# Layer-norm sums of tile 2 on ScalarE, the fourth input tile ahead of wv, and the last k norm in halves: one change to a fused attention and MLP kernel

## The chip, the core and the metric

The kernel runs on one core of one Trainium2 chip. The time is the device time of one launch in microseconds (us); the figure used is the median over several runs. An engine is called as in the profile: PE is TensorE (PEld its weight loads), DVE is VectorE, ACT is ScalarE, POOL is GpSimd, SP is SyncE, which here only issues DMAs.

## What is computed

The input x has 2048 tokens of 448 features in bf16. It is normalised, and two branches run on the normalised x:

```
xn  = layernorm(x)                                  # eps 1e-5, no scale or bias
# branch A, 16 heads of 28
q, k, v = split(xn @ wqkv)
phi(t)  = concat(softmax(t @ w_phi), softmax(-t @ w_phi))
kv = sum over tokens of phi(k)^T v ;  z = sum over tokens of phi(k)
A  = (phi(q) kv / (phi(q) z + 1e-6)) @ wo
# branch B
h  = gelu(layernorm(xn) @ w1)
hs = (h with its four column quarters shifted by -1, +1, -2, +2 tokens) @ w2
x1 = xn + hs
B  = x1 + gelu(layernorm(x1) @ w3) @ w4
out = x + A + B
```

Since xn is already normalised, the kernel uses it for both branches' first products.

## The kernel before

**Tiles.** The tokens are 16 tiles of 128. `xtok` holds x, `xn` the normalised x with tokens on the partitions, `xnT` its transpose with features on the partitions. The 448 features of a contraction lie in four overlapping chunks of 128, so that a matmul uses 64 rows of PE and two matmuls on the upper and the lower 64 rows run side by side; a "pair" below is such a couple. Where the upper rows write a bank after the lower rows did, PE waits for its own earlier matmul.

**Order.** Nothing is scheduled automatically. A `Recorder` notes every operation in the order of the program, gives each engine its own instruction queue in that order, and sets semaphores where a tile is written and read. So the order in which lines are written is the order on each engine's queue. Helpers record the operations, so most rows of the profile carry a helper's line: L200 is a matmul, L204 a PE transpose, L208 an ACT instruction with one output, L212 an element-wise instruction, L215 a transposing DMA, L218 a DMA, L807 a sum on ACT.

**Loads (L354 to 364).** x tiles 0, 2 and 3 are issued by SP, tile 1 by ACT; then the two halves of `wv` (the v columns of wqkv, contraction chunks 0, 1 and 2, 3), the first by ACT and the second by SP; then the further x tiles, two or four at a time, `w1`, `w_phi` and transposing loads of wqkv, all on SP.

**Head (L794 to 830).** A tile is normalised in steps: mean and variance by `ln_stats` (bn_stats and bn_aggr on DVE); the variance plus eps; to the power -1/2 on POOL (`ln1_pow`); and one DVE instruction that subtracts the mean and multiplies (`ln1_apply`). Tile 1 is treated otherwise: ACT forms the mean (Copy with a running sum) and the mean square (Square with a running sum) by `ln1_sum`, DVE computes mean squared minus eps, POOL subtracts it from the mean square, then the power. PE meanwhile runs `spin`: matmuls of 256 columns on constant data whose result is not used, 18 ahead of the transposes of tile 0 and 5 behind them. `xn_T(i, b)` transposes tile i by eight small matmuls into bank pair b, and ACT (for some tiles DVE) copies the result to `xnT`.

**First part of v (L534 to 555, L869).** `v_pair(i, b)` computes v for tiles i and i+1. It returns three steps: early (index 0), late (1) and mid (2). `V(i, 0)` is one pair of matmuls of chunk 0, `V(i, 2)` the other three, `V(i, 1)` the six matmuls that cross over to the other bank; for i above 3 the early step holds the mid step too. The order on PE is: tile 2's transposes, V(0,0), tile 3's transposes, V(0,2), V(0,1), V(2,0), V(2,2), then the first products with w1.

**Norm of k (L634 to 646) and kv (L648, L662, L667).** For a couple of tiles, `k_norm` sums the exponentials of each head on DVE, takes the reciprocal, and POOL multiplies all of both tiles in one instruction over 128 x 1792 (L643). The last call, for tiles 14 and 15, first has DVE apply the second layer norm to tiles 4 and 5 (`g_apply`, and after the norm `g_T`, a transposing DMA). `kv_tile(i)` is 16 matmuls of 62 columns on PE that add tile i to kv in banks 6 and 7. `kv_copy` (DVE) folds the two banks, `kv_blocks` (PE, then DVE and ACT) lays kv out for the products with phi(q).

**Later part (L930 to 985).** A list written by hand interleaves steps on PE: `a(p)` and `b(p)` are the early (8 matmuls of 512 columns) and late (6) half of a product with w3, followed by a gelu on ACT; `K(...)` calls kv_tile; `w2_last` finishes the last product with w2; `N(i)` multiplies phi(q) of tile i with kv; `f(n, k)` are the steps of the final product; `S` stores; `A` and `G` call g_apply and g_T. The part of interest reads:

```
a(0), (wl[11][0],), b(0), a(1), K(10, 11), b(1), K(12), a(2), K(13), b(2), a(3), K(14, 15), b(3), (kv_copy,),
a(4), (w2_last, 11), b(4), a(5), (kv_blocks,), b(5),
a(6), N(0), ...
```

Of the kernel before, what the change touches and what calls it, by code (L numbers as in the profile page):

```python
# [5 lines left out]
ACT = mybir.ActivationFunctionType  # L6
ALU = mybir.AluOpType
# [4 lines left out]
LN_EPS = 1e-5  # L12
# [208 lines left out]
def bass_parallel_sum__linear_kernel_hedgehog__mixer_s_mlp__prompt_kernel(  # L221
    nc, A_x, A_wqkv, A_w_phi, A_wo, B_x, B_w1, B_w2, B_w3, B_w4, out,
):
    _, S, D = A_x.shape
    H, DH = A_w_phi.shape[0], A_w_phi.shape[1]
# [10 lines left out]
    with es:  # L236
        R = Recorder(nc, es)
# [9 lines left out]
        def view(h, cols, dt=BF16, at=0):  # L247
            a = h[:, at // 2:at // 2 + cols * DTB[dt] // 2]
            return a if dt == BF16 else a.bitcast(dt)

        def new(name, cols, dt=BF16):
            return view(region(name, cols * DTB[dt]), cols, dt)
# [9 lines left out]
        xtok = new("xtok", NT * D).rearrange("p (t d) -> p t d", t=NT)  # L262
# [14 lines left out]
        wv = new("wv", KC * D).rearrange("p (c d) -> p c d", c=KC)  # L277
# [11 lines left out]
        g_tok = view(g_r, 4 * 512).rearrange("p (b d) -> p b d", b=4)  # L289
# [8 lines left out]
        st = new("st", NT * 8, F32).rearrange("p (t c) -> p t c", t=NT)  # L298
        mv = new("mv", NT * 8, F32).rearrange("p (t c) -> p t c", t=NT)
        rs = new("rs", NT * 8, F32).rearrange("p (t c) -> p t c", t=NT)  # L300
        st2 = new("st2", NT * 8, F32).rearrange("p (t c) -> p t c", t=NT)
# [38 lines left out]
        dve, pool = "DVE", "POOL"  # L340


        def load_x(i, n, eng="SP"):
            R.dma(xtok[:, i:i + n, :], x2d[128 * i:128 * (i + n), :].rearrange("(j p) d -> p j d", p=128), eng)
# [5 lines left out]
        def load_lap(dst, src, engs=("SP", "SP")):  # L350
            for h in range(2):
                R.dma(dst[:, 2 * h:2 * h + 2, :], src[192 * h:192 * h + 256, :].rearrange("(c p) d -> p c d", p=128), engs[h])
# [1 line left out]
        load_x(0, 1)  # L354
        load_x(1, 1, "ACT")
        load_x(2, 1)
        load_x(3, 1)
        load_lap(wv, A_wqkv[:, 896:1344], ("ACT", "SP"))
        load_x(4, 2)
        load_x(6, 2)  # L360
        load_lap(w1, B_w1)
# [66 lines left out]
        def lap(a):  # L428
            return bass.AP(a.tensor, a.offset, [list(a.ap[0]), [192, 2], [1, 256]])

        def halves(a):
            return a.rearrange("p (b e) -> p b e", b=2)

        def ln_stats(stt, mvt, src, i):
            R.ew(dve, "bn_stats", stt[:, i, 0:6], src[:, i, 0:D])
            R.ew(dve, "bn_aggr", mvt[:, i, 0:2], stt[:, i, 0:6])
# [8 lines left out]
        def ln_apply(eng, dst, src, mvt, rst, i):  # L445
            m, op = (mvt[:, i, 0:1], ALU.subtract) if eng == dve else (rst[:, i, 1:2], ALU.add)
            R.ew(eng, "tensor_scalar", dst, src, m, rst[:, i, 0:1], op0=op, op1=ALU.mult)
# [6 lines left out]
        def ln1_apply(eng, i):  # L454
            ln_apply(eng, halves(xn[:, i, :]), lap(xtok[:, i, :]), mv, rs, i)
# [3 lines left out]
        def spin(n, cols):  # L459
            for _ in range(n):  # L460
                R.mm(banks[7][:, 0:cols], busy[:, 0:128], busy[:, 0:cols], True, True)
# [49 lines left out]
        LO, HI = (0, 64), (64, 128)  # L511

        def row_pairs(first, second, start=False, cols=1):
            for s, (p, q) in enumerate(zip(first, second)):
                for out, lhs, rhs in (p, q) if cols == 1 else (*p, *q):
                    R.mm(out, lhs, rhs, start and s == 0, False)
# [17 lines left out]
        def v_pair(i, b):  # L534
            def side(k, rows, kcs):
                lo, hi = rows
                return [(banks[2 * b + k][:, 0:D], xnT[lo:hi, kc, 128 * (i + k):128 * (i + k) + 128], wv[lo:hi, kc, :])
                        for kc in kcs]

            def early():  # L540
                row_pairs(side(0, LO, (0,)), side(1, HI, (0,)), True)
                if i > 3:
                    mid()

            def mid():
                row_pairs(side(0, LO, (1, 2, 3)), side(1, HI, (1, 2, 3)))
            return early, lambda: row_pairs(side(1, LO, (0, 1, 3)), side(0, HI, (0, 2, 3))), mid

        def v_out(i, b, eng="ACT"):
# [56 lines left out]
        def w2_pair(i, b):  # L606
            def side(k, j, rows):
                lo, hi = rows
                t, r = i + 4 * j, []
                for c in range(3):  # L610
                    c0 = HB + 128 * t - SHIFTS[lo > 0][c]
                    r.append((banks[2 * b + j][:, 0:D], hT[lo:hi, c, c0:c0 + 128], w2[lo:hi, c, :]))
                if k:
                    c0 = 128 * (t % 4) + 2
                    r.append((banks[2 * b + j][:, 0:D], hD[lo:hi, t // 8, c0:c0 + 128], w2[lo:hi, 3, :]))
                return r
            return (lambda: row_pairs(side(1, 0, LO), side(1, 1, HI), True),
                    lambda: row_pairs(side(0, 1, LO), side(0, 0, HI)))
# [15 lines left out]
        def k_norm(i, between=()):  # L634
            ph = phik[:, i:i + 2, :, 0:DH].rearrange("p t g e -> p (t g) e")
            r = 2 * (i // 2 % 2)
            k, rk = (t[:, r:r + 2, :].rearrange("p b c -> p (b c)") for t in (ksum, rks))
            R.ew(dve, "tensor_reduce", k, ph, axis=AX.X, op=ALU.add)
            R.ew(dve, "reciprocal", rk, k)
            for j in between:  # L640
                g_apply(j, dve)
            rb = rk.unsqueeze(2).to_broadcast([128, 4 * H, DH])
            R.op(pool, lambda e: e.tensor_tensor(ph, ph, rb, op=ALU.mult), [ph],  # L643
                 [ph, rk, *(g_tok[:, j % 4, :] for j in between)])
            for j in between:
                g_T(j)

# [34 lines left out]
        def g_apply(i, eng="POOL"):  # L682
            ln_apply(eng, halves(g_tok[:, i % 4, :]), lap(xn[:, i, :]), mv2, rs2, i)

        def g_T(i):
            j = 128 * (i % 4)
            R.dma_t(gT[:, (i // 4) % 2, :, j:j + 128], g_tok[:, i % 4, :])
# [106 lines left out]
        def play(fs):  # L794
            for f in fs:
                f[0](*f[1:])

        def ln1_pow(j, at):
            R.ew(pool, "tensor_tensor", rs[:, j, 0:1], mv[:, j, at:at + 1], mhalf[:, 0:1], op=ALU.pow)

        def ln1_eps(j):
            R.ew(dve, "tensor_scalar", mv[:, j, 2:3], mv[:, j, 1:2], LN_EPS, 1.0, op0=ALU.add, op1=ALU.mult)
            ln1_pow(j, 2)

        def ln1_sum(j, func, scale, acc, junk):
            out, in_ = xn[:, junk, 0:D], xtok[:, j, :]
            R.op("ACT", lambda e: e.activation(out, in_, func, scale=scale, accum_out=acc), [out, acc], [in_])  # L807

        sq = st2[:, 1, 0:1]
        ln1_sum(1, ACT.Copy, 1.0 / D, mv[:, 1, 0:1], 14)  # L810
        ln1_sum(1, ACT.Square, D ** -0.5, sq, 15)
        ln_stats(st, mv, xtok, 0)
        ln1_eps(0)
        R.ew(dve, "tensor_scalar", mv[:, 1, 2:3], mv[:, 1, 0:1], mv[:, 1, 0:1], -LN_EPS, op0=ALU.mult, op1=ALU.add)
        R.ew(pool, "tensor_tensor", mv[:, 1, 4:5], sq, mv[:, 1, 2:3], op=ALU.subtract)
        ln1_pow(1, 4)
        ln_stats(st, mv, xtok, 2)
        ln1_apply(dve, 0)
        ln1_eps(2)
        ln_stats(st, mv, xtok, 3)  # L820
        ln1_apply(dve, 1)
        ln1_eps(3)
        ln1_apply(dve, 2)
        ln1_apply(dve, 3)
        spin(18, 256)
        play([(xn_T, 0, 0), (spin, 5, 256), (xn_T, 1, 1)])
        for i in range(4, 10):
            ln1_stats(i, 1, 0)
            if i > 4:
# [63 lines left out]
        side = [12, 0, 1, 2, 3, 8, 9, 10]  # L893
# [34 lines left out]
        wl = {i: w2_pair(i, 2) for i in (11,)}  # L928

        def a(p):  # L930
            return (w3p[p][0],)

        def b(p):
            return (w3p[p][1],)

        def f(n, k):
            return (fp[k][n - 1],)

        def N(i):
            return (lambda: (num_tile(i), o_T(i)),)  # L940

        def K(*t):
            return (lambda: [kv_tile(i) for i in t],)
# [5 lines left out]
        def G(*t):  # L949
            return (lambda: [g_T(i) for i in t],)  # L950
# [4 lines left out]
        def A(*t):  # L955
            return (lambda: [g_apply(i) for i in t],)

        play([
            (ln_scale, mv2, rs2, 6, 2, 0), (g_apply, 6, dve), (g_apply, 7, dve), G(6, 7),
            a(0), (wl[11][0],), b(0), a(1), K(10, 11), b(1), K(12), a(2), K(13), b(2), a(3), K(14, 15), b(3), (kv_copy,),  # L960
            a(4), (w2_last, 11), b(4), a(5), (kv_blocks,), b(5),
            a(6), N(0), (w2_norm, 8), b(6), a(7), f(1, 0), b(7), N(1), (w2_norm, 10), A(8, 9, 10, 11),
            a(8), f(2, 0), b(8), G(8, 9), a(9), N(2), (w2_norm, 12), b(9),
            a(10), f(3, 0), b(10), f(4, 0), G(10, 11),
# [51 lines left out]
```

The softmax here doesn't subtract the row's maximum and nothing guards it: scores larger than these inputs give would overflow.

## Time and profile before

| what | us |
|---|---|
| median of 5 runs | 174.1 (174.07 to 174.38) |
| the profiled execution's own time | 174.07 |
| its span (first to last instruction) | 172.3 |
| around the span | 1.8 |
| busy PE / DVE / POOL / ACT | 168.0 / 111.9 / 91.2 / 83.3 |
| first real transposes on PE (tile 0) | 5.55 |
| transposes of tiles 1, 2, 3 | 6.67, 7.05, 7.90 |
| V(0,0), V(0,2), V(0,1) start | 7.18, 8.03, 8.83 |
| POOL's norm of k tiles 14 and 15 | 71.32 to 74.53 |
| K(14, 15) on PE | 74.59 |

Times in the profile count from the start of the span. A row gives the start, the length, the engine, the line of the kernel, the operation, the tile written and the tiles read, the shapes, how many instructions of the kind follow one another, and, in brackets, how long the engine stood idle before and what ended that. The matmuls of PE are pipelined and their ends are modelled, so neighbouring rows overlap; starts are the safer figure. [...]

### The profile page before, as it was taken

What the parts mean: (1) busy time and instruction counts of PE and PEld (TensorE: products, weight loads), DVE (VectorE), ACT (ScalarE), POOL (GpSimd) and SP (SyncE); (2) the same over time, 40 slices, a digit from 0 to 9 for tenths busy, and PEclk for the clock granted to TensorE, in tenths of its full rate; (3) what the DMA queues carried; (4) which work ended last, traced back from release to release, by engine and by line L of the source; (5) the groups of instructions that cost most, each with busy time, mean ns of one, the idle gap of its engine ahead of it and who ended that gap; (6) DMA issues with size and microseconds to landing.
All of it is one profiled execution on the core that took longest, in us unless ns stands there. A gap on an engine that the chain in (4) does not pass through costs nothing.

```text
span 172.3 us, 5209 instructions
## 1 busy us (share of the span) xinstructions
PE 168.0 (98%) x2267; PEld 89.7 (52%) x2267; DVE 111.9 (65%) x260; ACT 83.3 (48%) x98; POOL 91.2 (53%) x128
## 2 busy tenths in 40 slices
PE   7899999999999999999999999999999999999994
PEld 5455576544555554544545555545545555545553
DVE  4899975278999999846677963446417425474621
ACT  4568874988778877847225322224204222224000
POOL 3576570025799999750649389540721614523740
PEclk9999999999999999999999999999999999999999
DMA  5994642229942011122103732034411220313331
GB/s 158 346 226 79 130 105 50 46 42 382 376 139 55 13 30 30 34 46 49 30 4 66 90 63 60 27 88 99 87 30 55 61 57 4 84 30 34 84 88 53
DMA packets 32679, 15.21 MB, mean 88 GB/s; under 512 B 23952, under 2 KB 32016, under 8 KB 32656
## 3 DMA queue, kind: packets, MB, share of 16 engines
q1 hardware_dynamic: 32096, 14.51, 34.3%
q8 instruction: 18, 0.29, 0.7%
q10 hardware_dynamic: 560, 0.37, 0.7%
q14 instruction: 5, 0.04, 0.1%
HBM read 7.14 MB, written 1.84 MB: 52 GB/s over the span
## 4 chain that ended last, share of the span: by engine, by line
PE 94%; DVE 3%; issue 1%; ACT 0%
PE bank L200 93%; PE bank L204 1%; DVE st L212 1%; DVE vaug L212 1%; DVE mv L212 1%; ACT xnT L208 0%; DVE xn L212 0%; DVE gT L212 0%
## 5 line engine op out<-in xcount | busy, mean ns | idle before, releaser
L208 ACT ACTIVATE phik<-bank 128x1024 bf16<-128x1024 f32 (+1 forms) x44 | 42.3, 984 | 60.4 <-PE bank L200 60.3
L200 PE MATMUL bank<-gT,w 64*128 64x512 bf16 x392 | 50.0, 377 | 0.0
L212 DVE TENSOR_TENSOR vaug<-bank,vaug 128x464 f32<-128x464 f32 (+3 forms) x65 | 32.7, 512 | 22.5 <-PE bank L200 20.9
L200 PE MATMUL bank<-w,phik 64*128 64x448 bf16 (+3 forms) x434 | 45.2, 343 | 0.0
L212 POOL TENSOR_TENSOR xnT<-vaug 128x196 bf16<-128x196 f32 (+1 forms) x32 | 18.1, 586 | 45.8 <-DVE vaug L212 45.8
L200 PEld LDWEIGHTS bank<-w,phik 64*128 64x128 bf16 (+1 forms) x434 | 22.5, 94 | 20.8 <-issue 0.4
L643 POOL TENSOR_TENSOR phik<-phik,rks 128x1792 bf16<-128x1792 bf16 x8 | 25.6, 3215 | 11.1 <-DVE rks L212 10.3
L200 PEld LDWEIGHTS bank<-gT,w 64*128 64x128 bf16 x392 | 17.6, 94 | 17.5 <-ACT phik L208 0.4
L212 POOL TENSOR_TENSOR vaug<-xn,xtok 128x448 f32<-128x448 bf16 x16 | 16.2, 1032 | 0.2 <-DVE vaug L212 0.2
L212 DVE TENSOR_REDUCE ksum<-phik 128x64 f32<-128x1792 bf16 x8 | 16.1, 2012 | 0.0
L212 DVE RECIPROCAL vaug<-bank 128x16 f32<-128x16 f32 x16 | 4.1, 257 | 17.9 <-PE bank L200 17.9
L212 POOL TENSOR_TENSOR rs<-mv,mhalf 128x1 f32<-128x1 f32 (+2 forms) x20 | 13.2, 661 | 3.5 <-DVE mv L212 2.1
L200 PE MATMUL bank<-xnT,wpq 64*128 64x512 bf16 x112 | 14.7, 376 | 0.0
L200 PE MATMUL bank<-wv,xnT 64*128 64x448 bf16 x112 | 13.6, 350 | 0.2
L200 PE MATMUL bank<-wo,xnT 64*128 64x448 bf16 (+3 forms) x110 | 13.6, 343 | 0.0
L200 PE MATMUL bank<-w,hT 64*128 64x448 bf16 x112 | 13.2, 349 | 0.0
L200 PE MATMUL bank<-wpk,xnT 64*128 64x448 bf16 x112 | 13.2, 349 | 0.0
L200 PE MATMUL bank<-xnT,w 64*128 64x512 bf16 (+2 forms) x168 | 13.0, 306 | 0.0
L212 DVE TENSOR_TENSOR xn<-bank,xn 128x512 bf16<-128x512 f32 (+1 forms) x16 | 9.2, 620 | 2.9 <-PE bank L200 2.9
L212 DVE BATCH_NORM_STATS2 st<-xn 128x6 f32<-128x448 bf16 x16 | 9.3, 581 | 0.0
L212 POOL TENSOR_SCALAR g_tok<-xn,rs 128x512 bf16<-128x512 bf16 x12 | 9.1, 769 | 0.3
L212 DVE BATCH_NORM_STATS2 st<-xtok 128x6 f32<-128x448 bf16 x15 | 9.2, 615 | 0.0
(68 smaller groups left out, 162.9 us busy)
## 6 DMA issues: line engine op xcount, KB each, us to landing
w<-in_B_w_dram SPq DMA_DIRECT2D x2, 896.0 KB, 5.8
out_dram<-vaug SPq DMA_DIRECT2D x15, 112.0 KB, 1.9
w<-in_B_w_dram SPq DMA_DIRECT2D x1, 1568.0 KB, 11.2
xtok<-in_A_x_dram SPq DMA_DIRECT2D x2, 448.0 KB, 5.8
xtok<-in_A_x_dram SPq DMA_DIRECT2D x2, 224.0 KB, 4.2
w<-in_B_w_dram SPq DMA_DIRECT2D x2, 224.0 KB, 4.5
wo<-in_A_wo_dram SPq DMA_DIRECT2D x2, 224.0 KB, 6.9
xtok<-in_A_x_dram SPq DMA_DIRECT2D x3, 112.0 KB, 2.8
```

The costliest lines, as they stand in the source:

```text
L200: self.op("PE", lambda e: e.matmul(out, lhsT, rhs, start=start, stop=stop, skip_group_check=True), [out], [lhsT, rhs], tile=self._tile(lhsT))
L204: self.op("PE", lambda e: e.transpose(out, in_, ident), [out], [in_, ident], tile=self._tile(in_))
L208: self.op("ACT", lambda e: e.activation(out, in_, func, **kw), [out], [in_] + aps)
L212: self.op(eng, lambda e: getattr(e, name)(out, *args, **kw), [out], aps)
L643: R.op(pool, lambda e: e.tensor_tensor(ph, ph, rb, op=ALU.mult), [ph], [ph, rk, *(g_tok[:, j % 4, :] for j in between)])
```

## The change

Five edits:

- x tile 3 is issued by ACT as its second load; both halves of wv are issued by SP.
- The sums of tile 2 are formed on ACT, right behind those of tile 1; `ln_stats` of tile 2 goes. `ln1_var` collects the three steps that follow such sums. On DVE, tile 3's stats stand where tile 2's stood, and tile 2's step of `ln1_var` stands behind the apply of tile 1. The unused outputs of the four sums go to rows 12 to 15 of `xn`.
- 20 spins ahead of tile 0's transposes and 2 behind them, for 18 and 5.
- For V(0, .) and V(2, .), the early step holds chunks 0 and 1 (four matmuls), the mid step chunks 2 and 3. For the other couples the sequence of matmuls is unchanged.
- In the last `k_norm`, POOL's multiply is two instructions of 128 x 896, tile 14 and then tile 15. K(14) stays behind a(3); K(15) moves behind a(4), and kv_copy behind it.

```diff
-        load_x(3, 1)
-        load_lap(wv, A_wqkv[:, 896:1344], ("ACT", "SP"))
+        load_x(3, 1, "ACT")
+        load_lap(wv, A_wqkv[:, 896:1344])
...
             def early():
-                row_pairs(side(0, LO, (0,)), side(1, HI, (0,)), True)
+                row_pairs(side(0, LO, (0, 1)), side(1, HI, (0, 1)), True)
...
             def mid():
-                row_pairs(side(0, LO, (1, 2, 3)), side(1, HI, (1, 2, 3)))
+                row_pairs(side(0, LO, (2, 3)), side(1, HI, (2, 3)))
...
-            R.op(pool, lambda e: e.tensor_tensor(ph, ph, rb, op=ALU.mult), [ph],
-                 [ph, rk, *(g_tok[:, j % 4, :] for j in between)])
+            for h in ((slice(0, 2 * H), slice(2 * H, 4 * H)) if between else (slice(0, 4 * H),)):
+                R.op(pool, lambda e, h=h: e.tensor_tensor(ph[:, h, :], ph[:, h, :], rb[:, h, :], op=ALU.mult),
+                     [ph[:, h, :]], [ph[:, h, :], rk, *(g_tok[:, j % 4, :] for j in between)])
...
-        sq = st2[:, 1, 0:1]
-        ln1_sum(1, ACT.Copy, 1.0 / D, mv[:, 1, 0:1], 14)
-        ln1_sum(1, ACT.Square, D ** -0.5, sq, 15)
+        def ln1_sums(j):
+            ln1_sum(j, ACT.Copy, 1.0 / D, mv[:, j, 0:1], 13 + j)
+            ln1_sum(j, ACT.Square, D ** -0.5, st2[:, j, 0:1], 11 + j)
+
+        def ln1_var(j):
+            R.ew(dve, "tensor_scalar", mv[:, j, 2:3], mv[:, j, 0:1], mv[:, j, 0:1], -LN_EPS, op0=ALU.mult, op1=ALU.add)
+            R.ew(pool, "tensor_tensor", mv[:, j, 4:5], st2[:, j, 0:1], mv[:, j, 2:3], op=ALU.subtract)
+            ln1_pow(j, 4)
+
+        ln1_sums(1)
+        ln1_sums(2)
         ln_stats(st, mv, xtok, 0)
         ln1_eps(0)
-        R.ew(dve, "tensor_scalar", mv[:, 1, 2:3], mv[:, 1, 0:1], mv[:, 1, 0:1], -LN_EPS, op0=ALU.mult, op1=ALU.add)
-        R.ew(pool, "tensor_tensor", mv[:, 1, 4:5], sq, mv[:, 1, 2:3], op=ALU.subtract)
-        ln1_pow(1, 4)
-        ln_stats(st, mv, xtok, 2)
+        ln1_var(1)
+        ln_stats(st, mv, xtok, 3)
         ln1_apply(dve, 0)
-        ln1_eps(2)
-        ln_stats(st, mv, xtok, 3)
         ln1_apply(dve, 1)
+        ln1_var(2)
         ln1_eps(3)
         ln1_apply(dve, 2)
         ln1_apply(dve, 3)
-        spin(18, 256)
-        play([(xn_T, 0, 0), (spin, 5, 256), (xn_T, 1, 1)])
+        spin(20, 256)
+        play([(xn_T, 0, 0), (spin, 2, 256), (xn_T, 1, 1)])
...
-            a(0), (wl[11][0],), b(0), a(1), K(10, 11), b(1), K(12), a(2), K(13), b(2), a(3), K(14, 15), b(3), (kv_copy,),
-            a(4), (w2_last, 11), b(4), a(5), (kv_blocks,), b(5),
+            a(0), (wl[11][0],), b(0), a(1), K(10, 11), b(1), K(12), a(2), K(13), b(2), a(3), K(14), b(3),
+            a(4), K(15), (kv_copy,), (w2_last, 11), b(4), a(5), (kv_blocks,), b(5),
```

## The prediction

> **What bounds the kernel now.** I read the page first: busy shares, then the chain that ended last, then the waits of TensorE and of its weight loads, then each engine's instructions in order of time in the two stretches that the diff touches.
>
> ```profile
> PE 168.0 (98%) x2267; PEld 89.7 (52%) x2267; DVE 111.9 (65%) x260; ACT 83.3 (48%) x98; POOL 91.2 (53%) x128
> PE 94%; DVE 3%; issue 1%; ACT 0%
> 8.83 2.36 PE bank L200 x22
> 26.11 143.93 PE bank L200 x1900
> ```
>
> TensorE (PE) is 98% busy, the chain is 94% PE, and after 8.83 us it is PE without a break. From there every microsecond that PE loses or saves moves the end. Before 8.83 PE waits for the first four token tiles to be normalised; the chain there runs through VectorE (DVE), GpSimd (POOL) and the copies of ScalarE (ACT). The change touches that head and one short place at 74 us. The head, engine by engine:
>
> ```profile
> 4.42 0.56 POOL L212 TENSOR_TENSOR rs<-mv,mhalf 128x1 f32<-128x1 f32 x1 [1.76 <-DVE mv L212]
> 4.95 0.19 POOL L212 TENSOR_TENSOR mv<-st,mv 128x1 f32<-128x1 f32 x1
> 5.21 0.70 POOL L212 TENSOR_TENSOR rs<-mv,mhalf 128x1 f32<-128x1 f32 x1
> 6.75 0.65 POOL L212 TENSOR_TENSOR rs<-mv,mhalf 128x1 f32<-128x1 f32 x1 [0.33 <-DVE mv L212]
> ...
> 5.48 0.62 DVE L212 BATCH_NORM_STATS2 st<-xtok 128x6 f32<-128x448 bf16 x1
> 6.23 0.38 DVE L212 TENSOR_SCALAR xn<-xtok,mv,rs 128x512 bf16<-128x512 bf16 x1
> 6.53 0.15 DVE L212 TENSOR_SCALAR mv<-mv 128x1 f32<-128x1 f32 x1
> 6.59 0.41 DVE L212 TENSOR_SCALAR xn<-xtok,mv,rs 128x512 bf16<-128x512 bf16 x1
> 7.44 0.41 DVE L212 TENSOR_SCALAR xn<-xtok,mv,rs 128x512 bf16<-128x512 bf16 x1 [0.44 <-POOL rs L212]
> ...
> 7.90 0.17 PEld L204 LDWEIGHTS bank<-ident,xn 64*128 64x128 bf16 x8 [0.16 <-DVE xn L212]
> 8.82 1.06 PEld L200 LDWEIGHTS bank<-wv,xnT 64*128 64x128 bf16 x14 [0.50 <-PE bank L200]
> ```
>
> (Start, length, engine, line, tiles; in brackets idle time before and who ended it.) Each tile needs a power on POOL (0.54 to 0.70) and an apply on DVE (0.38 to 0.41). Tile 3's apply (7.44 to 7.85) releases its transposes at 7.90, these release the six V matmuls of V(0,2) at 8.03, and V(0,1) must wait for those to drain: the last pair starts at 8.41, V(0,1) at 8.83, so a bank hand-over of 0.41. At 8.83 dense work starts, with 14 matmuls of tiles 0 to 3 still to do.
>
> **The head after the change.** DVE loses tile 2's bn_stats and bn_aggr, about 0.75 on its queue; ACT gains two sums. ACT is idle from 4.70 to 5.89; at the rows of tile 1 (0.56 each, with 0.19 to read a sum) the new pair ends at 5.80, just before its first copy at 5.89, so it costs nothing; without that gap it would push the copies by up to 1.1. Tile 3's stats move from 5.48 to 4.37, if x3 has landed: as third load of SP it took 3.4 from its issue at 1.72; as second of ACT at 1.26, beside x2 (2.8), I put it at 4.1 to 4.7. Behind bn_stats 3 stand only two short steps until 5.9, so 0.3 late costs nothing. wv's first half, now third on SP, lands 0.1 to 0.7 after its 4.46, and its first reader runs past 7. SP still issues four loads before x4, so nothing behind them on the two queues moves.
>
> The chain, with the gaps of the rows above: POOL's power of tile 1 stays at 5.21 to 5.91, since the subtraction before it and its cause do not change. Apply 1 follows 0.04 later: 5.95 to 6.33, where it was 6.23. That is a gain of 0.28 for tile 1. But tile 2's variance now stands behind apply 1 on DVE: its small multiply runs 6.25 to 6.40 (a start 0.09 before the end of the instruction ahead, as in the row at 6.53), POOL's subtraction 0.08 later, 6.48 to 6.67, its power 6.75 to 7.29 (0.54, no apply beside it). Queued behind that on POOL is tile 3's power, 7.26 to 7.92 (0.65, apply 2 beside it). On DVE, apply 2 runs 7.33 to 7.74, where it was 6.59 to 7.00, and apply 3 7.96 to 8.37 against 7.44 to 7.85. So the earlier stats of tile 3 buy nothing: POOL now does five steps in a row behind a DVE instruction that was not on the path before, and the last two tiles are late by 0.74 and 0.52.
>
> PE: transposes of tile 2 at 7.79, V(0,0) with four matmuls instead of two at 7.92, transposes of tile 3 at 8.42, V(0,2) with four at 8.55. Its second pair starts 0.19 later, 8.74, and the hand-over of 0.41 puts V(0,1) at 9.15. Behind it stand 6, 4 and 4 matmuls, 14 as before. The loss is 9.15 - 8.83 = **0.32**. The two matmuls moved ahead of tile 3 save 0.19 of the 0.52. With every power at 0.54 it is 0.22; with 0.70 for both late powers and some slower step, 0.50. I take 0.32: the rows with the same neighbours.
>
> DVE's later queue starts 0.51 late (bn_stats 4 at 7.76) while PE is 0.32 late. From 9.9 to 18.6 DVE has no pause, so the lag stays, but the smallest margin of a tile, apply 11 (ends 18.59) before its transposes at 19.14, is 0.55, above the 0.19 of difference. That costs nothing; with margin gone it would be 0.19.
>
> The spins: two more ahead, three fewer behind tile 0. The first 18 end at 5.28 and the first transposes start at 5.56. The spacing of the first is (4.02 - 0.42) / 17 = 0.21, so two more end at 5.70 at the worst and push tile 0 by 0.15, which tile 1's wait until 6.38 hides.
>
> **The kv part.**
>
> ```profile
> 71.32 3.21 POOL L643 TENSOR_TENSOR phik<-phik,rks 128x1792 bf16<-128x1792 bf16 x1 [0.85 <-DVE g_tok L212]
> 74.24 0.38 PE L200 MATMUL bank<-gT,w 64*128 64x512 bf16 x2
> 74.59 0.20 PE L200 MATMUL bank<-vaug,phik 64*128 64x62 bf16 x2
> 74.59 0.51 PEld L200 LDWEIGHTS bank<-vaug,phik 64*128 64x128 bf16 x32 [0.47 <-POOL phik L643]
> ```
>
> A pair of 512 columns takes 0.216 (74.02 to 74.24), so tiles 14 and 15 could start at 74.45 and start at 74.59: a stall of 0.14, ended by POOL's norm. In halves, tile 14's is done at about 71.32 + 1.61 = 72.93 and tile 15's at 74.5 to 74.7. K(14) then starts at 74.45; K(15), behind six and eight more matmuls, near 76.2. Both find their data. The second POOL instruction costs 0 to 0.1, and the scale behind it on POOL, the two g applies on DVE and their gT loads are as late; their readers come past 82. kv_copy, before at 76.28 behind those applies, now waits for K(15), whose last pair starts at 76.40: copy from about 76.63, its second half ends at 78.08, and the blocks are wanted at 78.3: 0.2 to spare. The two w2_out adds follow to 79.14, the CASTs that N(0) needs end at 79.9, N(0) loads at 80.03. The saving is **0.14**; if one of those two covers fails, 0 down to a loss of 0.1.
>
> **The sum.** 0.32 - 0.14 = 0.18 on a profiled run of 174.07 (span 172.3 and 1.8 around it), which is at the low end of the five times; on the median of 174.1 I get 174.3. With all ends: 0.22 - 0.15 = +0.07 to 0.50 + 0.1 = +0.6.
>
> **Rivals.**
>
> (1) PE's clock falls back. The spins of the first stretch are 0.21 apart, those at 5.78 (0.72 - 0.27) / 4 = 0.11: PE began at half pace and was fast from about 5.2. From 5.2 to 8.6 before, its array worked about 2.0 of 3.4: five spins 0.55, V 0.94, transposes 0.5. After the change I count 1.3: spins 0.37, V 0.43, transposes 0.5, with a hole from 6.5 to 7.79. If that is too little, PE runs at half pace again in the dense part. The first slow stretch lasted 3.95 from the first spin; half of it is lost, 2.0, of which about 0.3 lies beside waits (the hand-over at 8.8): 1.7. Time 176.0. For it: the thinner stretch, at the only place with such a hole. Against: no trace here shows how thin is too thin, and the granted clock stands at 1.00 throughout. It decides if the array's share between 5.2 and 8.6 is below the limit.
>
> [...]
>
> (2) The loss is absorbed. After 8.83 weight loads still wait for others, at 12.95 (0.15), 15.20 (0.44), 20.89 (0.17), 24.53 (0.29) and 26.64 (0.17). If those partners keep their times, a PE that comes 0.3 late waits 0.3 less there, and the kv gain stays alone: 174.1 - 0.14 = 173.95; with powers that run faster than their rows, or a stall at 74 that was larger than its 0.14, 173.7. Against: most partners are fed by PE itself and slide with it.
>
> (3) The head loses nothing at all because POOL takes tile 3's power ahead of tile 2's. The instruction order of the changed kernel rules it out: subtraction, power 2, power 3.
>
> **How the numbers follow.** A measurement of this kernel tells about 0.2%, 0.35 us, from no change. My forecast, a net of +0.05 to +0.6, gets 0.44: 0.24 of it below +0.35 and 0.20 above, since the ends of the head's terms lie on the slow side. The clock 0.34. The absorbed loss 0.22, half of it faster by 0.35 and half within. Faster 0.11, same 0.24 + 0.11 = 0.35, slower 0.20 + 0.34 = 0.54. The likeliest single case is 174.3, its own range 174.1 to 174.7; the whole range 173.8 to 176.1 takes in the clock.
>
> **What would show it.** Right: apply 2 near 7.3 and apply 3 near 7.95 with POOL before both, V(0,1) at 9.15, no wait at 74.5, kv_copy after K(15). Clock: pairs of 448 columns 0.37 apart instead of 0.19 somewhere past 8. Wrong: V(0,1) at or before 8.83 would fell the head's sum; a CAST that ends after 80.0, or a wait of N(0), would fell the kv gain.

## The result, and the profile after

| | before | after |
|---|---|---|
| median, us | 174.19 (173.94 to 176.14, 46 executions) | 175.61 (174.11 to 176.25, 26 executions) |
| ratio after / before, 95% interval | | 1.0052 (1.0035 to 1.0069) |
| profiled execution: own time / span / granted clock | 174.07 / 172.3 / 1.00 | 176.2 / 174.3 / 0.99 |

The change makes the kernel slower, by 0.35 to 0.69%. The median says little about how, because the 26 executions fall into two groups with nothing between. 11 took 174.11 to 174.42 (median 174.31) with PE's mean granted clock at 1.00. 15 took 175.57 to 176.25 (median 175.84) with the clock at 0.99. The ratio lies near that of the averages (175.19 against 174.28), as do the ratios below, which leave out the few executions over 1.5% above the fastest of their kernel; the median lies in the larger group. Of the 46 executions before, one is as long, and of the 91 of before that ran beside the experiments four show a clock of 0.99 or less: before does it too, but rarely. The profiled execution of after is one of the 15. The same parts of its page as were shown of before, and the row of the clock:

```profile
span 174.3 us, 5212 instructions
PE 169.0 (97%) x2266; PEld 90.1 (52%) x2266; DVE 111.5 (64%) x258; ACT 84.5 (48%) x102; POOL 91.5 (52%) x130
...
PEclk9969999999999999999999999999999999999999
...
PE 94%; DVE 2%; issue 1%; POOL 1%
```

PE still bounds the kernel, and its busy time has grown by 1.0 for the same work. The third slice of the clock, 8.7 to 13.1, reads 6: for part of it, up to 11.45, PE was granted half its pace (0.50 in the clock record). Now the head, engine by engine (columns as in the prediction):

```profile
5.27 0.70 POOL L212 TENSOR_TENSOR rs<-mv,mhalf 128x1 f32<-128x1 f32 x1
...
6.62 0.19 POOL L212 TENSOR_TENSOR mv<-st,mv 128x1 f32<-128x1 f32 x1 [0.65 <-DVE mv L212]
6.89 1.06 POOL L212 TENSOR_TENSOR rs<-mv,mhalf 128x1 f32<-128x1 f32 x2
...
5.68 0.19 ACT L808 ACTIVATION_READ_ACCUMULATOR xn<-xtok 128x1 f32 x1
5.95 0.60 ACT L208 ACTIVATE xnT<-bank 128x512 bf16<-128x512 bf16 x1
...
6.01 0.41 DVE L212 TENSOR_SCALAR xn<-xtok,mv,rs 128x512 bf16<-128x512 bf16 x1 [0.45 <-POOL rs L212]
6.34 0.27 DVE L212 TENSOR_SCALAR mv<-mv 128x1 f32<-128x1 f32 x2
7.47 0.93 DVE L212 TENSOR_SCALAR xn<-xtok,mv,rs 128x512 bf16<-128x512 bf16 x2 [0.87 <-POOL rs L212]
...
7.94 0.35 PE L204 MATMUL bank<-ident,xn 64*128 64x64 bf16 x8 [1.18 <-DVE xn L212]
10.06 0.13 PEld L200 LDWEIGHTS bank<-wv,xnT 64*128 64x128 bf16 x4 [0.86 <-PE bank L200]
```

POOL stands idle for 0.65 until DVE, behind apply 1 (6.01), has multiplied tile 2's mean (6.34). Then it forms both late powers in one row (6.89, two in 1.06), and the applies of tiles 2 and 3 follow as one row from 7.47 to 8.40. PE has nothing for 1.18 before tile 2's transposes at 7.94. V(0,1) starts only at 10.06, after a hand-over that took 0.86 instead of 0.50.

The windows view gives, for a stretch of time: its length; busy time of PE, PEld, DVE, ACT and POOL with the number of instructions; granted clock; DMA share; GB/s. Of after:

```profile
4.60:8.00 3.40, 1.60 (x28) 0.81 (x27) 1.94 (x8) 2.46 (x8) 2.55 (x6) 1.00 1.05 335
8.00:11.40 3.40, 3.34 (x32) 1.33 (x34) 3.07 (x9) 1.19 (x2) 1.53 (x5) 0.51 1.22 338
11.40:14.80 3.40, 3.40 (x52) 1.75 (x48) 3.30 (x10) 2.47 (x4) 2.67 (x7) 0.99 0.59 106
```

and of before:

```profile
4.60:8.00 3.40, 2.73 (x41) 1.29 (x40) 2.89 (x11) 1.70 (x5) 2.40 (x5) 1.00 1.06 349
8.00:11.40 3.40, 3.33 (x49) 1.60 (x48) 3.07 (x9) 1.65 (x4) 2.00 (x6) 1.00 1.22 285
```

After a stretch in which PE was busy for 1.60 of 3.40 (2.73 before), it ran at clock 0.51 for the next 3.4: 32 matmuls, where before did 49 in that stretch and after did 52 in the 3.4 behind it. In the trace's clock record the half pace lasts from 8.04 to 11.45. (The rows that start at 4.60 flatter before: its clock rose at 5.21, that of after at 4.62, and up to there spins started 0.21 apart, behind it 0.11. The section on the prediction counts the work itself.) The kv part of after:

```profile
73.21 3.35 POOL L644 TENSOR_TENSOR phik<-phik,rks 128x896 bf16<-128x896 bf16 x2 [0.85 <-DVE g_tok L212]
...
76.14 0.48 PEld L200 LDWEIGHTS bank<-vaug,phik 64*128 64x128 bf16 x16
76.58 1.19 PEld L200 LDWEIGHTS bank<-gT,w 64*128 64x128 bf16 x14
77.89 0.48 PEld L200 LDWEIGHTS bank<-vaug,phik 64*128 64x128 bf16 x16
...
78.53 0.68 DVE L212 COPY w<-bank 128x496 f32<-128x496 f32 x1
80.97 0.79 DVE L212 CAST kvq<-bank 32x232 bf16<-32x232 f32 x2
```

The halves take 3.35 together, against 3.21 in one, and neither K(14) nor K(15) has idle time ahead of it.

**The sum of the profiled execution.** Tile 0's bn_stats, which need x0, did not start at the same time in the two executions (3.30 before, 3.35 after), so the head is counted from there.

| step, from the starts of the rows | change, us |
|---|---|
| later start of tile 0's bn_stats | +0.05 |
| to the first product with w1 (6.86 before, 8.71 after) | +1.85 |
| from there to the first product with w3 | 0.00 |
| from the first product with w3 to K(14) (7.29, 7.16) | -0.13 |
| wait for a transposed o tile late in the run, 160.78 below | +0.33 |
| sum, against 172.16 - 170.06, the starts of the last instruction on DVE | +2.10, against +2.10 |

The first products with w1, of before and of after, and the wait late in after:

```profile
10.16 1.03 PE L200 MATMUL bank<-xnT,w 64*128 64x512 bf16 x8
12.06 1.02 PE L200 MATMUL bank<-xnT,w 64*128 64x512 bf16 x8
...
160.78 0.49 PEld L200 LDWEIGHTS bank<-wo,xnT 64*128 64x128 bf16 x7 [0.42 <-DMA xnT<-xnT]
```

This last wait differs between executions: the transposing DMA of that tile took 4.4 to land here, 4.2 in experiment 3 (a wait of 0.2), 3.7 in before and 3.2 in experiment 1, whose products did not wait. Of the 1.85, the next section shows 0.31 to be the lateness of tiles 2 and 3 and 1.54 the half pace.

### The profile page after: what moved, and what is told of

Read it like the earlier page. It is cut to its first block, busy times and chain, and to the rows that moved or that the text cites. A ratio compares the mean times of both kernels' runs of the same rounds, so it can differ in the third digit from the quotient of the medians.

```text
span 174.3 us, 5212 instructions
## 1 busy us (share of the span) xinstructions
PE 169.0 (97%) x2266; PEld 90.1 (52%) x2266; DVE 111.5 (64%) x258; ACT 84.5 (48%) x102; POOL 91.5 (52%) x130
## 4 chain that ended last, share of the span: by engine, by line
PE 94%; DVE 2%; issue 1%; POOL 1%
PE bank L200 93%; PE bank L204 1%; POOL rs L212 1%; DVE vaug L212 1%; DVE xn L212 0%; DVE mv L212 0%; DVE st L212 0%; POOL mv L212 0%; DVE gT L212 0%
## 5 line engine op out<-in xcount | busy, mean ns | idle before, releaser
L644 POOL TENSOR_TENSOR phik<-phik,rks 128x1792 bf16<-128x1792 bf16 (+1 forms) x9 | 25.8, 2876 | 11.1 <-DVE rks L212 10.3
L212 POOL TENSOR_TENSOR rs<-mv,mhalf 128x1 f32<-128x1 f32 (+2 forms) x20 | 13.1, 657 | 3.3 <-DVE mv L212 1.8
L200 PE MATMUL bank<-wv,xnT 64*128 64x448 bf16 x112 | 14.7, 380 | 0.1
L208 ACT ACTIVATE hT<-bank 128x512 bf16<-128x512 f32 (+1 forms) x10 | 7.3, 768 | 3.4 <-PE bank L200 3.4
```

The lines of the kernel that those rows point to most:

```text
L200: self.op("PE", lambda e: e.matmul(out, lhsT, rhs, start=start, stop=stop, skip_group_check=True), [out], [lhsT, rhs], tile=self._tile(lhsT))
L208: self.op("ACT", lambda e: e.activation(out, in_, func, **kw), [out], [in_] + aps)
L212: self.op(eng, lambda e: getattr(e, name)(out, *args, **kw), [out], aps)
L644: R.op(pool, lambda e, h=h: e.tensor_tensor(ph[:, h, :], ph[:, h, :], rb[:, h, :], op=ALU.mult), [ph[:, h, :]], [ph[:, h, :], rk, *(g_tok[ ...
```

## The experiments

Two theories were set against each other. *Lateness*: after loses because tiles 2 and 3 come late, and PE's pace has nothing to do with it or depends on chance. *Thin stretch*: between the fast spins and tile 2's transposes PE has too little work, which costs it the full pace for one stretch of 3.4 (8.04 to 11.45 in after's clock record). V(0,1) below is counted from the start of tile 0's bn_stats: 5.53 before, 6.71 in after.

**1. Fill the hole.** After, with spins behind tile 1's transposes:

```diff
-        play([(xn_T, 0, 0), (spin, 2, 256), (xn_T, 1, 1)])
+        play([(xn_T, 0, 0), (spin, 2, 256), (xn_T, 1, 1), (spin, 8, 256)])
```

> The changed kernel with eight more unused matmuls (spins) between the transposes of tiles 1 and 2, in the wait from 6.6 to 7.9. Theory (thin stretch lets the clock fall): PE's array work in the 3.4 us before the fall rises from 1.0 us by about 0.9 to the 1.9 to 2.0 of the kernel before, PE keeps its full clock in all or nearly all executions, and the time is 174.2 to 174.4, where the changed kernel's executions lie that kept the clock. Rival (the clock fell for another reason, or the long times come from waits in the late head): about half of the executions stay at 175.6 to 176.2 and the median stays near 175.6.

Measured: 174.21 (174.06 to 174.38, 11 executions), clock 1.00 in all; before beside it 174.15; ratio 1.0 (0.9991 to 1.0009). Its windows:

```profile
4.60:8.00 3.40, 3.10 (x42) 1.79 (x41) 1.94 (x8) 2.37 (x7) 2.44 (x6) 1.00 1.02 324
8.00:11.40 3.40, 3.33 (x54) 1.49 (x49) 3.07 (x10) 2.03 (x3) 1.64 (x5) 1.00 1.25 333
```

DVE did the same as in after (1.94 and 3.07), but PE got through 54 matmuls in the second stretch, not 32. V(0,1) stands at 5.84, the first product with w1 at 7.17, both 0.31 later than before: that is the lateness, and the other 1.54 of the 1.85 was the pace. Eight matmuls without use bring back all that the larger group lost.

**2. Make before thin.** The five spins behind tile 0 go, nothing else:

```diff
-        play([(xn_T, 0, 0), (spin, 5, 256), (xn_T, 1, 1)])
+        play([(xn_T, 0, 0), (xn_T, 1, 1)])
```

> The kernel before with the five spins behind tile 0's transposes left out and nothing else changed (their result is not used). Theory: the array's work from 5.2 to 8.6 drops from 1.95 to about 1.4 of 3.4, nearer to the changed kernel's 1.0; in a part of the executions the clock falls and those take 175.6 to 176.2, while the others stay at 174.1. If the limit lies below 1.4, all stay at 174.1. Rival (spins only fill a wait and the fall comes from the change's own instructions): 174.1 to 174.2 in all executions.

Measured: 175.37 (173.86 to 176.85, 12 executions), ratio 1.0051 (1.0028 to 1.0073). Six executions took 175.3 to 175.7 at clock 0.99, where 3 of the 35 executions of before beside them had 0.99 or less; two more are long at full clock. The head's dates are those of before in the profiled one (V(0,1) at 5.53), which kept the clock. None of the six was profiled: that their fall lies in the head is argued from the edit, which changes nothing else, and not shown by a trace. So a thin stretch did it without any lateness, and it did not take a long hole: the longest idle time of PE in this head is

```profile
6.52 0.67 PE L204 MATMUL bank<-ident,xn 64*128 64x64 bf16 x16 [0.72 <-DVE mv L212]
```

**3 and 4. The two halves of the change.** The kv edits alone on before (L643 in halves, K(15) and kv_copy moved), and after with these undone. Of the edit only the list is shown; the halves of L643 are those of the change:

```diff
-            a(0), (wl[11][0],), b(0), a(1), K(10, 11), b(1), K(12), a(2), K(13), b(2), a(3), K(14, 15), b(3), (kv_copy,),
-            a(4), (w2_last, 11), b(4), a(5), (kv_blocks,), b(5),
+            a(0), (wl[11][0],), b(0), a(1), K(10, 11), b(1), K(12), a(2), K(13), b(2), a(3), K(14), b(3),
+            a(4), K(15), (kv_copy,), (w2_last, 11), b(4), a(5), (kv_blocks,), b(5),
```

> The kernel before with the kv part of the change alone (last k norm in halves, K(15) behind a(4)). Theory: the stall of 0.14 at 74.5 is gone and nothing else moves: 0.14 faster than before, about 174.0 to 174.05, full clock. Rival (the late copy of kv makes a new wait at N(0)): no gain or up to 0.1 slower, with a wait of PE in front of N(0).

> The changed kernel with the kv part undone: its head alone. Theory: two groups of executions, as in the changed kernel, each about 0.14 longer: near 174.5 with the full clock (0.32 more than before) and near 175.8 to 176.3 with a fall of the clock, about half of each. Rival (the kv part carries some of the loss): the head alone is at most 0.1 slower than before where the clock holds.

Measured: the kv edits 174.08 (173.78 to 174.31, 12, clock 1.00 in all), ratio 0.9988 (0.9974 to 1.0002); K(14) comes 0.13 earlier after the first product with w3 and N(0) waits for nothing. The head alone 175.74 (173.96 to 176.14, 12), ratio 1.0042 (1.0004 to 1.008): five executions at 173.96 to 174.46 with clock 1.00 and seven at 175.69 to 176.14 with 0.99. The two groups are the head's doing. Its full-clock group lies lower than expected (median 174.31, as in after). In the profiled one V(0,1) is at 5.70, since there tile 1's power took 0.56 and not 0.70; that this holds for the others is not shown.

**5 and 6. Take the lateness away, then fill as well.** In after, tile 2's variance and tile 3's eps go ahead of apply 1, so that POOL never waits behind it:

```diff
         ln1_apply(dve, 0)
-        ln1_apply(dve, 1)
         ln1_var(2)
         ln1_eps(3)
+        ln1_apply(dve, 1)
```

> The changed kernel with tile 2's variance step and tile 3's eps step ahead of apply 1 on DVE instead of behind it. Theory (the head is late because POOL's power of tile 2 waits for a multiply queued behind apply 1): power 2 starts at about 6.2 instead of 6.9, apply 2 near 6.9 and apply 3 near 7.5 instead of 7.5 and 8.0 (counted from tile 0's stats at 3.35); V(0,1) comes 5.3 after the first stats, where the kernel before has 5.53 and the changed kernel with full clock 5.84. Executions that keep the clock: 173.75 to 173.95. But the stretch before V is still thin, so some executions should fall to half pace and take about 1.5 more. Rival (POOL is bound by its own five steps): apply 2 and 3 move by less than 0.2 and executions with the full clock stay at 174.3.

Measured: 173.81 (173.56 to 177.25, 12), ratio 0.9979 (0.995 to 1.0007), clock 1.00 in all; 9 executions lie at 173.56 to 173.92, and two are over 175 without a fall of the clock. POOL of this kernel:

```profile
5.92 0.19 POOL L212 TENSOR_TENSOR mv<-st,mv 128x1 f32<-128x1 f32 x1
6.19 1.06 POOL L212 TENSOR_TENSOR rs<-mv,mhalf 128x1 f32<-128x1 f32 x2
```

The subtraction runs at 5.92 (6.62 in after) and V(0,1) stands at 5.24: 0.29 earlier than before, 0.60 earlier than with the order of after. The falls of clock that were expected here did not come: with tiles 2 and 3 earlier, real work fills more of the stretch (PE busy 2.83 of the 3.40 from 4.60, a part of it spins still at half pace).

The next kernel adds spins to it:

```diff
-        play([(xn_T, 0, 0), (spin, 2, 256), (xn_T, 1, 1)])
+        play([(xn_T, 0, 0), (spin, 4, 256), (xn_T, 1, 1), (spin, 4, 256)])
```

> As e5, with four spins behind tile 0 and four behind tile 1 instead of two and none. Theory: no fall of the clock, all executions at 173.75 to 173.95, which is 0.2 to 0.4 faster than before. Rival: as long as the sums on ACT are there, the head is not shorter than before, 174.1 or more.

Measured: 175.41 (173.6 to 177.27, 12), ratio 1.0027 (0.9992 to 1.0062). A miss, for a reason at another place. V(0,1) is at 5.27, as good as before the spins, but PE waits here:

```profile
28.33 1.01 PEld L200 LDWEIGHTS bank<-xnT,w 64*64 64x64 bf16 x39 [1.81 <-DMA xnT<-xn]
```

The transposing DMAs of tiles 12 and 13 were issued by SP at 22.10 and 23.42 (21.32 and 22.59 before), behind the loads of w2, and took 4.2 to 4.9 to land (2.4 to 3.3 before). Three of the twelve executions also show clock 0.99; none of them was profiled, so whether that followed the same wait is open.

**7 and 8. The spins apart from the order.** After with the old spins (18 and 5), and before with the new ones (20 and 2):

```diff
-        spin(20, 256)
-        play([(xn_T, 0, 0), (spin, 2, 256), (xn_T, 1, 1)])
+        spin(18, 256)
+        play([(xn_T, 0, 0), (spin, 5, 256), (xn_T, 1, 1)])
```

> The changed kernel with the old spins, 18 and 5. Theory: the wait from 6.5 to 7.9 stays empty and the array works about 0.2 more in the thin stretch (1.2 instead of 1.0 of 3.4): the clock still falls in a part of the executions, rather fewer than the 15 of 26 of the changed kernel. Rival (the spin counts alone are to blame): all executions keep the clock and take 174.2 to 174.4, as with the filled wait.

> The kernel before with the new spins, 20 and 2, and nothing else. Theory: the stretch holds about 1.6 of array work, between the 1.8 of the kernel before and the 1.3 to 1.4 with no spins behind tile 0: few falls or none, most executions at 174.1. Rival (the spin counts alone are to blame): about half at 175.5 to 176.2.

Measured: after with the old spins 174.26 (173.88 to 175.51, 12), one fall of the clock, ratio 1.0001 (0.9977 to 1.0024), V(0,1) at 5.84; before with the new spins 174.09 (173.93 to 174.19, 12), no fall, ratio 0.9986 (0.9967 to 1.0004), V(0,1) at 5.54. So the fewer spins alone (0 of 12) and the later tiles alone (1 of 12) cost the pace rarely, as rarely as in before within what such counts tell; both together cost it in 15 of 26.

**9, 10 and 11. The loads of w2 moved back.** To free SP for the transposing DMAs, the three w2 loads were moved to where the last loads are issued, in kernel 5, in before, and in kernel 6:

```diff
-        R.dma(w2[:, 0:3, :], B_w2[0:384, :].rearrange("(c p) d -> p c d", p=128))
-        for p0 in (0, 64):
-            R.dma(w2[p0:p0 + 64, 3, :], B_w2[384:448, :])
...
+            R.dma(w2[:, 0:3, :], B_w2[0:384, :].rearrange("(c p) d -> p c d", p=128))
+            for p0 in (0, 64):
+                R.dma(w2[p0:p0 + 64, 3, :], B_w2[384:448, :])
```

> As e5 (tile 2's step ahead of apply 1), with the three loads of w2 moved from SP's queue ahead of the transposing DMAs of tiles 12 and 13 to behind the halo copies, ahead of w3. Theory: the executions that took 1 to 2 more at full clock waited at 26 to 28 us for these two DMAs, which stood behind the w2 loads (in the profile of e6 1.8 of wait). With the queue free they start at DVE's apply instead, 0.4 to 1 earlier, and all executions lie at 173.5 to 174.0; w2 is first used near 45. Rival (the late landing has nothing to do with the queue): the spread stays as in e5 and e6, some executions at 174.8 to 176.

> The kernel before with only the w2 loads moved, as in e9. Theory: in most executions nothing changes (174.1, the DMAs start at 21.3 with DVE's apply either way), but those at 174.5 to 175.5 with full clock become rarer. Rival: w2 lands too late for its first product or pushes the halo copies: slower than 174.2.

> As e6 (e5 with four and four spins) with the w2 loads moved. Theory (e6's long executions come from the late DMAs, not from the spins): all at 173.5 to 174.0 with the full clock. Rival (the spins themselves cost, or the clock falls in spite of them): the median stays above 174.5.

Measured: 181.71, 181.16 and 179.61 (6 executions each), ratios 1.0455 (1.041 to 1.0501), 1.0385 (1.0358 to 1.0413) and 1.031 (1.0283 to 1.0338). The place was too late: w2's first product is due at 36.5 in before, and in before with that edit w2 is issued at 37.05. PE and the windows of this kernel:

```profile
40.66 2.26 PE L200 MATMUL bank<-w,hT 64*128 64x448 bf16 x8 [3.86 <-DMA w<-in_B_w_dram]
```

```profile
38.00:42.00 4.00, 1.34 (x7) 0.48 (x7) 0.00 (x0) 0.27 (x1) 3.14 (x1) 0.71 0.82 211
42.00:46.00 4.00, 3.94 (x21) 1.61 (x22) 0.00 (x0) 1.73 (x2) 0.00 (x0) 0.50 1.02 399
46.00:50.00 4.00, 4.00 (x39) 1.78 (x37) 3.18 (x4) 2.40 (x3) 0.00 (x0) 0.94 1.09 379
```

The wait is 3.86, the loss 7.1 (181.16 against 174.1). The clock tells where much of the rest went: 0.71, 0.50 and 0.94, so a half pace after the wait too, with 21 matmuls in 4.0 against 39. In the clock record it lasts from 39.66 to 46.49, twice 3.41. Of that 5.83 lie behind the wait, and half of them, 2.9, make 6.8 with the wait. In the three profiles the DMAs of tiles 12 and 13 landed within 3.8 and nothing waited for them.

**12. The loads of w2 in the middle.** Kernel 6, the three loads directly behind the transposing DMAs of tiles 12 and 13 (only the new place is shown):

```diff
             for i in (12, 13):
                 xn_Td(i)
+            R.dma(w2[:, 0:3, :], B_w2[0:384, :].rearrange("(c p) d -> p c d", p=128))
+            for p0 in (0, 64):
+                R.dma(w2[p0:p0 + 64, 3, :], B_w2[384:448, :])
```

> As e6 (tile 2's step ahead of apply 1, four and four spins), with the three w2 loads directly behind the transposing DMAs of tiles 12 and 13 on SP's queue instead of directly ahead of them; the first halo copies wait for them, by up to 1.7, which their own wait for ACT until 31 covers. Theory (e6's long executions come from these two DMAs starting late behind w2, not from the spins): no wait of PE for them at 26 to 28, nearly all executions at 173.5 to 174.0 with the full clock, faster than both kernels. Rival (the DMAs land late by themselves, or the spins cost): the median stays above 174.5 as in e6. If w2 lands too late: a wait at the first product with w2 near 36.

Measured: 173.66 (173.5 to 174.03, 6 executions), clock 1.00 in all; before on the same chip 174.42 (174.21 to 174.93); ratio 0.9957 (0.994 to 0.9974). The wait of 1.81 is gone:

```profile
26.33 1.12 PEld L200 LDWEIGHTS bank<-xnT,w 64*64 64x64 bf16 x40 [0.17 <-ACT hT L208]
```

V(0,1) stands at 5.24. This kernel is faster than before, by 0.26 to 0.60%, and so than after. Its six executions are few, and before was at 174.10 to 174.19 in the other series, so the gain may lie near the lower end. It keeps the change's sums, loads, matmul order and kv edits, and differs from after in the order of tile 2's variance, in the spins and in the place of the w2 loads.

## Why the prediction was right or wrong

The direction that it gave most of the chance, slower, is what came, and the time lies in its range. But its likeliest single case, 174.3 at full clock, describes 11 of the 26 executions, and rival (1), at 176.0, the other 15 and with them the median. That the median is 175.6 and not 174.3 hangs on 15 against 11, which nothing in the prediction could tell. Step by step:

- **Head: the path right, its closeness in part luck.** Tile 2's variance stood behind apply 1 and POOL did both late powers behind it. Apply 2 came at 7.47 (7.33 forecast, and this head began 0.05 late), so 0.09 later than forecast; but tile 3's power took 0.55 in spite of apply 2 beside it, not 0.65, and apply 3 came at 7.99 (7.96). The two misses cancel. Where the clock held (experiment 1), V(0,1) was late by 0.31 against the 0.32 of the sum.
- **Sums on ACT: right.** They end at 5.87, and the first copy starts at 5.95, as late as its tile.
- **kv: right.** 0.13 saved of the forecast 0.14, in after and by itself in experiment 3; kv_copy, 1.90 later like all around it, fell at 78.53 (76.63 + 1.90), and N(0) did not wait. The second POOL instruction cost 0.14 (3.35 against 3.21), above its 0 to 0.1, and nothing waited for that.
- **The sum at full clock: right, within what can be told.** Forecast +0.18; the medians give +0.12 (174.31 against 174.19), and experiment 1 +0.06 with an interval around no change.
- **Spins at nothing: wrong.** The term weighed two more and three fewer spins only as a delay. It is the step that failed: with after's late tiles, 20 and 2 in place of 18 and 5 moved the falls of clock from 1 execution in 12 to 15 in 26, and the medians from 174.26 to 175.61. The cover was not a wait but work that kept the pace.
- **Rival (1): its mechanism right, its size near, its chance too low.** Price forecast 1.7; measured 1.54 in the profile and 1.53 between the two groups' medians (175.84 - 174.31). Two parts were off: the slow stretch was put at 3.95 and lasted 3.41, and 0.3 was put down as lying beside waits, where half of 3.41 less 1.54 leaves 0.17. Neither the stretch of 3.4 in which it counted the work nor a limit on that work is shown by the trace of before: both were the author's estimate. After's clock record has a full-pace stretch of 3.41 (4.62 to 8.04) with little work, and behind it one of 3.41 at half pace. Its count of the work left in the thin stretch, 1.3, was high: 0.97 in the stretch ahead of the fall. That the clock of before stood at 1.00 throughout was counted against it; it was no evidence, since before had more work at that place.
- **Rival (2): wrong.** Nothing was absorbed: in experiment 1 the first product with w3 is still 0.31 late.

The falls needed no long gap: the longest ahead of the fall in after's profile was 1.18, and in experiment 2, a head whose longest gap was 0.72 in the profiled execution, 6 of 12 executions lost the pace.

How thin is too thin is bounded, not settled. Counting each matmul of a profile as its columns at its pace (the 256 columns of a spin in 0.11 at full and 0.21 at half pace), and transposes like the others, which no run here tests, the least work of PE's array in any 3.41 of the head is 0.96 in after's profile (which fell), 1.32 in kernel 7 (1 of 12 fell), 1.50 in kernel 2 (6 of 12), 1.56 in kernel 4 (7 of 12), 1.73 in kernel 8 (0 of 12), 1.82 in before (4 of 91) and 1.98 or more in kernels 1, 5 and 12 (none). Low values go with falls, but kernel 7 breaks the order, and each figure is from one execution: after and kernel 4 have the same head, yet 0.96 and 1.56, as have kernels 5 and 9, yet 1.98 and 1.56.

The clock records of the profiles suggest why. In each, every change lies a whole number of steps of 3.413 behind the first rise: 4.62, 8.04, 11.45 and 175.29 (48 steps more) in after; 5.21 and 172.46 (49 steps) in before; 5.53, 39.66 (10 steps) and 46.49 (2 more) in kernel 10. That looks as if the pace were judged in fixed stretches of 3.413, and where these lie against the program differed from execution to execution: the first rise came between 4.62 and 6.07 in the eleven profiles that have such a record. In the stretch that starts with the rise the work is 0.97 in after, where it just holds the hole, 1.68 in kernels 4 and 7, and 1.76 or more in the other eight. Only after's was followed by half pace. A limit between 0.97 and 1.68, an estimate from these figures, fits all eleven, and which executions of a kernel fall would then be the chance of where the stretches lie. Only one of these profiles shows a fall in the head, so this is argued, not shown.

Two things were not tried: x3 ahead of wv, and the sums on ACT, each alone. Why kernel 6 took over 174.8 so much more often than kernel 5, with the same queue on SP, is not settled either; only one of its long executions was profiled.

## What to carry to other kernels

Matmuls whose result nobody uses can be what keeps PE at full pace: eight of them took after from 15 falls of the clock in 26 executions to none in 11. Before they are cut, or before real work beside them is made later, add up what PE does in each stretch of the length of the half pace (3.41 here), and if it falls clearly below what the kernel had (0.96 in after against 1.82 here), fill it. When times form two groups, compare the granted clock of the groups (0.99 and 1.00 here) before looking for an edit's cost in instructions, and judge by a count of executions, not by one profile. And when work that was bound by an order on another engine becomes late, look first for a small instruction queued behind a large one: here one line moved was worth 0.60 at V(0,1).

## What the runs showed that was not expected

- The granted clock fell for one stretch of 3.41 (8.04 to 11.45 in after) and was back after it, without any long idle time of PE ahead of it (1.18 at the most); and it fell in some executions of a kernel and not in others (15 of 26 of after). The clock rose between 4.62 and 6.07 after the start of the span where a record shows it, and in kernel 12, which has none, spins were 0.11 apart from 4.2 on, so its rise came at another place in the program from one execution to the next.
- A long wait cost more than itself: in experiment 10, 3.86 of waiting for w2 were followed by 5.83 at half pace.
- The transposing DMAs of tiles 12 and 13 took 2.4 to 4.9 to land in these profiles, and 0.8 of later issue behind other loads on SP went with a wait of 1.81 on PE.
